# Attention scores as plain fp32 products of 64 rows, two units per visit, with mask and row maximum in one instruction

## The chip, the core and the metric

The kernel runs on one core of a Trainium2 chip. Five engines work side by side, each through its own queue in order: TensorE (PE, with weight loads listed apart as PEld), VectorE (DVE), ScalarE (ACT), GpSimd (POOL) and SyncE (SP), which here only issues DMAs. The metric is the device time of one execution in microseconds; the time given is the median of several.

## The reference

Sparse attention over 8 batches, 8 heads, 576 positions and 64 head dimensions, then a gated feed-forward layer on the 4608 tokens that result (512 to 1536 to 512):

```python
scores = scale * np.matmul(q, k.transpose(0, 1, 3, 2))        # scale = 1/8
mask_local = (rel >= 0) & (rel < 32)                          # heads 0-3
mask_strided = (rel >= 0) & (pos[None, :] % 32 == pos[:, None] % 32)   # heads 4-7
scores = np.where(masks, scores, -1000000000.0)
attn = np.exp(scores - np.max(scores, axis=-1, keepdims=True))
attn = attn / (np.sum(attn, axis=-1, keepdims=True) + 1e-09)
x = np.matmul(attn, v)                                        # tokens x 512
rms = np.sqrt(np.mean(x * x, axis=-1, keepdims=True) + 1e-06)
xn = x / rms * rms_g
g = xn @ w_gate
return (g * (1.0 / (1.0 + np.exp(-g))) * (xn @ w_val)) @ w_out
```

Everything is fp32.

## The kernel before

**Work.** The feed-forward layer goes through the tokens in nine chunks of 512: chunks 0 to 6 one at a time, the last two together by another scheme of products (lines 1190 to 1590). For one chunk, each of twelve slices of 128 hidden columns takes products for the gate (`g`), for the value (`v`) and for the output (`acc`), with 512 tokens as moving columns. A large fp32 product is written as three products in a rounded fp32 type, high times high, low times high and high times low (lines 970 and 1027); the two parts of each operand are made by a cast (`hi`) and a subtraction (`lo`).

**Attention.** The masks leave blocks only. A pair of heads is cut into three units, 96 units in all (`wus`, line 450; `o` is the number of the pair, three units to a pair, four pairs to a batch). A unit has two tiles, or one, for each of its two heads: local heads have tiles of 96 queries by 128 keys, strided heads tiles of 126 by 126 or 108 by 108. A unit runs through `step_s` (scores on PE, mask and row maximum on DVE, exponential on ACT, normalising on POOL), `step_t` (transposing, for most units on DVE in blocks of 32) and `step_o` (times the values on PE, then copies into `raw`, from which a chunk takes its tokens). Units 0 to 14 come in a prologue; from unit 15 on a unit is started with each slice of the chunk before, so that attention is spread between the large products.

**Scores before.** Two forms matter. Units 12 to 26 (line 653) multiply plain fp32 operands of 64 rows, the first head on rows 0 to 63 and the second on rows 64 to 127. From unit 27 on (`FP`, line 638) the operands are taken apart first: `split` (line 515) makes, for each pair of heads, six casts (line 540, ACT) and four subtractions (line 545, DVE) into the buffer `qk`, so that one product of 128 rows and 256 columns in the rounded type gives two of the three parts side by side. DVE then adds the mask to the first half (lines 674, 678), adds the second half (line 680) and takes the row maximum (line 681). For units 15 to 26 it adds the mask for each head (line 684) and takes the maximum (line 686).

**Buffers.** The buffer `qk` of `QKN` elements is also the place of three of the five slots for queries and keys (`xx`, line 387) until unit 27; after that there are only two slots, and each pair's scores come from `qk`. `pbuf` (the probabilities) has `NPB` = 2 buffers. Scores, transposes and values share one pair of PSUM banks, `pair`.

**Order.** Nothing is written in the order in which it runs. `op(...)` records an operation with its engine, cost, due time, and what it reads and writes; `Plan.order` (line 201) makes a schedule from the costs in two passes with the parameters `PASS_A` and `PASS_B` (`SWITCH` says where the second takes over), and each engine's instructions are emitted in that order. `also=` lists other engines that may take an operation, so a planner's choice can move work between DVE, POOL and ACT.

Of the kernel before, what the change touches and what calls it, by code (L numbers as in the profile page):

```python
# [343 lines left out]
def attn_moe(ctx: ExitStack, tc: tile.TileContext, qT: bass.AP, kT: bass.AP, vl: bass.AP, vs: bass.AP,  # L344
# [170 lines left out]
    def split(o, at):
        first = 3 * o == FP

        def part(fn, src, key, more=()):
            ways = [("ACT", act(S), False), ("DVE", 375, True)] if not more else [("DVE", 780, True), ("Pool", pool(S), True)]
            if "g" not in ALT:  # L520
                ways = ways[:1]
            op(*ways[0][:2], at, fn, reads=[("xx", src)] + list(more), writes=[key], port=ways[0][2], also=ways[1:])

        def begin():
            lw = sb.tile([P, QKN], F32R, name="qk")
            qk["q"] = lw[:, 0:2 * S].rearrange("p (h s) -> p h s", h=2)
            qk["k"] = lw[:, 2 * S:QKN].rearrange("p (h w s) -> p h w s", h=2, w=2)
            for h in range(2):
                for a, e in ((0, PAD), (SW, KP)):
                    z2 = ident[:, 0:2 * (e - a)].rearrange("p (w s) -> p w s", w=2)  # L530
                    nc.scalar.activation(out=qk["k"][:, h, :, a:e], in_=z2, func=AF.Copy, scale=0.0)
                r = (BOT, TOP)[h]
                nc.scalar.activation(out=qk["k"][r, h, 1, PAD:SW], in_=xx[1][r, PAD:SW], func=AF.Copy, scale=0.0)
        if first:
            op("ACT", 1800, at, begin, reads=[("xx", 1), "ident"],
               writes=low_keys + [(n, h, w) for n in "qk" for h in range(2) for w in range(3)])

        def copy(eng, d, s):
            if eng == "ACT":
                nc.scalar.copy(out=d, in_=s)  # L540
            else:
                (nc.gpsimd if eng == "Pool" else nc.vector).tensor_copy(out=d, in_=s)

        def sub(eng, d, s, y):
            (nc.gpsimd if eng == "Pool" else nc.vector).tensor_tensor(out=d, in0=s, in1=y.bitcast(F32), op=ALU.subtract)  # L545
        for h in range(2):
            r, z = ((TOP, BOT), (BOT, TOP))[h]
            q, k = (lambda r, h=h: qk["q"][r, h]), (lambda r, w, h=h: qk["k"][r, h, w, PAD:SW])
            x, y = xx[0][r, PAD:SW], xx[1][r, PAD:SW]
            part(lambda e, q=q, x=x, r=r: copy(e, q(r), x), 0, ("q", h, 0))  # L550
            part(lambda e, q=q, x=x, r=r, z=z: sub(e, q(z), x, q(r)), 0, ("q", h, 1), [("q", h, 0)])
# [1297 lines left out]
```

## Time and profile before

| | before |
|---|---|
| runs, us | 1011.88, 1016.63, 1017.29 (median 1016.63) |
| profiled execution, us | 1014.29, of which the span from first to last instruction is 1012.5 |
| mean granted TensorE clock | 0.994 |
| mean DMA rate over the span | 120 GB/s |

A group line of the profile gives line, engine, operation, what is written and read, shapes and count, then the busy time in us and the mean of one in ns, then the idle time of the engine just before. A timeline line gives the start and length in us, and in brackets how long the engine had been idle and who ended it. Matmuls overlap, so the length of one says little; the distance from one start to the next is its cost.

### The profile page before, as it was taken

How to read it: one execution, taken by the hardware profiler on the slowest of the kernel's cores; microseconds unless marked ns; L12 is line 12 of the kernel's file. 1: busy time of each engine (PE TensorE's matmuls, PEld its weight loads, DVE VectorE, ACT ScalarE, POOL GpSimd, SP SyncE). 2: the span in 40 equal slices, each digit the busy share in tenths (PEclk: the TensorE clock that was granted, in tenths of full speed). 3: DMA queues.
4: the chain of work that ended last, by engine and by line, in shares of the span. 5: the costliest groups of instructions: out<-in, count | busy, mean ns of one | idle time of the engine just before them, and what ended most of it. 6: DMA issues, size and time to landing. Idle time of an engine off the chain costs nothing.

```text
span 1012.5 us, 15391 instructions
## 1 busy us (share of the span) xinstructions
PE 992.7 (98%) x5104; PEld 805.4 (80%) x5104; DVE 846.3 (84%) x1745; ACT 572.1 (57%) x1502; POOL 416.6 (41%) x390
## 2 busy tenths in 40 slices
PE   8899998999999999999999999999999999999998
PEld 7678776788878888888878888887888878888886
DVE  5699999898889797779888888888987798888891
ACT  7899857655755456456555555555655444344440
POOL 6232457324562333533325342267643343565300
PEclk9899999999999999999999999999999999999999
DMA  9876342532442331433232432234322101120552
GB/s 310 294 271 225 134 138 96 169 116 85 159 146 81 114 122 60 166 99 112 92 120 91 136 114 98 88 122 140 108 91 79 42 0 42 42 84 1 158 165 73
DMA packets 52559, 121.11 MB, mean 120 GB/s; under 512 B 5312, under 2 KB 21248, under 8 KB 52480
## 3 DMA queue, kind: packets, MB, share of 16 engines
q1 hardware_dynamic: 51712, 119.28, 35.3%
q10 hardware_dynamic: 768, 0.85, 0.3%
q8 instruction: 40, 0.66, 0.3%
q14 instruction: 39, 0.32, 0.1%
HBM read 98.09 MB, written 22.02 MB: 119 GB/s over the span
## 4 chain that ended last, share of the span: by engine, by line
PE 81%; DVE 12%; ACT 4%; issue 2%; DMA 1%; DVEq 0%; ACTq 0%
PE g L970 18%; PE v L970 18%; PE acc L1027 18%; PE g L1356 3%; PE pair L1356 3%; PE v L1356 3%; PE pair L782 3%; PE pair L638 3%; DVE qk L545 2%; PE acc L1356 2%; PE g L1521 2%; PE v L1521 2%; PE acc L1521 2%; DVE raw L918 1%; DVE pT L745 1%
## 5 line engine op out<-in xcount | busy, mean ns | idle before, releaser
L970 PE MATMUL g<-xh,wg 128*128 128x512 f32 x672 | 211.8, 396 | 4.4 <-DVE e L985 4.4
L970 PE MATMUL v<-xh,wv 128*128 128x512 f32 x664 | 208.4, 395 | 1.8 <-DVE e L996 0.9
L1027 PE MATMUL acc<-or,hh 128*128 128x512 f32 x672 | 208.7, 392 | 0.0
L1012 POOL TENSOR_TENSOR hl<-e,hh 128x512 fp32r<-128x512 f32 x84 | 115.3, 1372 | 216.8 <-ACT hh L1003 196.4
L693 ACT ACTIVATE pp<-pp,mx 96x128 f32<-96x128 f32 (+2 forms) x296 | 114.2, 390 | 74.5 <-DVE mx L681 60.7
L702 POOL TENSOR_TENSOR pp<-pp,mx 96x512 f32<-96x512 f32 (+3 forms) x87 | 88.3, 1017 | 156.4 <-DVE mx L699 106.3
L970 PEld LDWEIGHTS g<-xh,wg 128*128 128x128 f32 x672 | 122.4, 189 | 31.1 <-DVE e L985 5.0
L1027 PEld LDWEIGHTS acc<-or,hh 128*128 128x128 f32 x672 | 124.4, 188 | 26.5 <-ACT ssq L1038 0.4
L970 PEld LDWEIGHTS v<-xh,wv 128*128 128x128 f32 x664 | 121.9, 189 | 28.7 <-DVE e L996 2.6
L970 PE MATMUL g<-xl,wg 128*128 128x512 f32 x336 | 131.9, 393 | 0.2 <-POOL xl L946 0.2
L1027 PE MATMUL acc<-or,hl 128*128 128x512 f32 x336 | 130.9, 390 | 0.0
L970 PE MATMUL v<-xl,wv 128*128 128x512 f32 x332 | 129.6, 390 | 0.0
L745 DVE STREAM_TRANSPOSE pT<-pp 32x128 f32<-32x128 f32 (+1 forms) x376 | 109.7, 292 | 11.9 <-POOL pp L702 6.9
L1003 ACT CAST hh<-e 128x512 fp32r<-128x512 f32 x84 | 52.4, 624 | 89.5 <-PE acc L1027 80.5
L983 ACT ACTIVATE e<-g 128x512 f32<-128x512 f32 x84 | 50.1, 597 | 78.6 <-PE g L970 64.4
L540 ACT CAST qk<-xx 64x576 fp32r<-64x576 f32 x138 | 88.8, 670 | 5.3 <-PE pair L638 3.8
L545 DVE TENSOR_TENSOR qk<-xx,qk 64x576 fp32r<-64x576 f32 x92 | 83.0, 902 | 6.3 <-ACT qk L540 3.8
L985 DVE SCALAR_TENSOR_TENSOR e<-e,g 128x512 f32<-128x512 f32 x84 | 57.4, 683 | 27.4 <-ACT e L983 26.5
L970 PEld LDWEIGHTS g<-xl,wg 128*128 128x128 f32 x336 | 63.4, 189 | 14.6 <-POOL xl L946 0.6
L1027 PEld LDWEIGHTS acc<-or,hl 128*128 128x128 f32 x336 | 63.1, 188 | 13.5
L970 PEld LDWEIGHTS v<-xl,wv 128*128 128x128 f32 x332 | 62.5, 188 | 13.4
L996 DVE SCALAR_TENSOR_TENSOR e<-e,v 128x512 f32<-128x512 f32 x83 | 56.9, 685 | 14.5 <-PE v L970 10.5
(515 smaller groups left out, 1804.7 us busy)
## 6 DMA issues: line engine op xcount, KB each, us to landing
or<-wos SPq DMA_DIRECT2D x72, 512.0 KB, 3.3
xx<-in_qT_dram SPq DMA_DIRECT2D x26, 288.0 KB, 2.8
xx<-in_kT_dram SPq DMA_DIRECT2D x25, 288.0 KB, 3.9
wg<-in_wgv_dram SPq DMA_DIRECT2D x12, 512.0 KB, 9.6
vt<-in_vl_dram SPq DMA_DIRECT2D x16, 384.0 KB, 3.2
wv<-in_wgv_dram SPq DMA_DIRECT2D x12, 512.0 KB, 7.4
or<-in_wo_dram SPq DMA_DIRECT2D x12, 512.0 KB, 4.2
wos<-or SPq DMA_DIRECT2D x12, 512.0 KB, 3.0
```

Of the source, the lines that this page charges most:

```text
L540: nc.scalar.copy(out=d, in_=s)
L545: (nc.gpsimd if eng == "Pool" else nc.vector).tensor_tensor(out=d, in0=s, in1=y.bitcast(F32), op=ALU.subtract)
L693: nc.scalar.activation(out=pv[:, h, x], in_=sp[h][:, x] if i < PM else pv[:, h, x], func=AF.Exp, scale=0.125 if i < PM else 1.0, bias=mx[: ...
L702: (nc.vector if e == "DVE" else nc.gpsimd).tensor_tensor(out=pv, in0=pv, in1=mx.unsqueeze(3).broadcast_to([m, 2, nt, n]), op=ALU.mult)
L745: nc.vector.transpose(out=dst[32 * y:32 * y + 32, :, 32 * x:32 * x + 32], in_=src[32 * x:32 * x + 32, :, 32 * y:32 * y + 32])
L970: nc.tensor.matmul(out=out, lhsT=wt[:, w, sl], rhs=xhl[x, kc], start=(kc == 0 and i == 0), stop=(kc == KC - 1 and i == 2))
L985: op("DVE", dve(CH), at + MO, lambda: nc.vector.scalar_tensor_tensor(out=e, in0=e, scalar=1.0, in1=bank["g"], op0=ALU.add, op1=ALU.mult), ...
L996: op("DVE", dve(CH), at + MO, lambda: nc.vector.scalar_tensor_tensor(out=e, in0=e, scalar=0.5, in1=bank_of(c, ("v", u))[0], op0=ALU.mult, ...
L1012: (nc.vector if n == "DVE" or h else nc.gpsimd).tensor_tensor(out=hl[h], in0=e, in1=hh[h].bitcast(F32), op=ALU.subtract)
L1027: nc.tensor.matmul(out=acc[t], lhsT=x[h][:, sl], rhs=wt[:, w], start=(u == 0 and i == 0), stop=(u == NU - 1 and i == 2))
L1356: nc.tensor.matmul(out=banks[bk], lhsT=w, rhs=X[a, k].tile(y), start=start and k == 0 and i == 0, stop=stop and k == 1 and i == 2, skip_gr ...
L1521: nc.tensor.matmul(out=banks[bks[j]], lhsT=tile(v, k, j), rhs=x.tile(y), start=start and k == 0 and i == 0, stop=stop and k == KT - 1 and ...
```

## The change

Units from 27 on no longer take their operands apart. `FP` is 99 and the code behind it is gone: `split`, the buffer `qk`, the products of line 638, the three or four DVE instructions of lines 674 to 681. All units from 12 on use the products of line 653 (line 604 after). From unit 28 (`BT`) on, two units are scored in one visit of PE: the second's scores stand in columns 256 to 511 of the two banks, and the visit therefore also takes the bank halves of transposes and values (`("T", 0)`).

For units from 15 on, mask, scale, and row maximum are one `tensor_tensor_reduce` for each head and tile. It computes -0.125 times the sum of score and mask (the mask is 0 or -1e9, so it stays far below all scores after the scaling) and keeps the minimum, which is the negative of the row maximum; the exponential then runs with scale -1.

The slots for queries and keys become six buffers of their own, `pbuf` has four, the last pair of chunks places its operands in `xx2` to `xx5` and `pp2`, `pp3` where it had `qk`, and planner numbers differ.

```diff
+TTRC = 135.0
+SC0 = 272.0
-FP = 27
+FP = 99
+BT = 28
-BA = 30000.0
-BM = 60000.0
+BA = 10000.0
+BM = 20000.0
-NPB = 2
+NPB = 4
-PASS_A = ([25.0, 0.0, 150.0, 50.0], 0.2, 8000.0, 12)
-PASS_B = ([25.0, 600.0, 300.0, 400.0], 0.2, 12000.0, 5)
-SWITCH = 220000.0
+PASS_A = ([25.0, 0.0, 150.0, 37.5], 0.3, 4000.0, 8)
+PASS_B = ([25.0, 900.0, 225.0, 300.0], 0.2, 4000.0, 7)
+SWITCH = 180000.0
...
-    low = sbt([P, QKN], "qk")
-    xx = [sbt([P, SW], f"xx{i}") for i in range(2)] + [low[:, SW * i:SW * i + SW] for i in range(3)]
+    xx = [sbt([P, SW], f"xx{i}") for i in range(6)]
...
-            starts[s] = [i]
+            starts.setdefault(s - (i >= BT and (i - BT) % 2), []).append(i)
...
     def slot_of(o, x):
-        return x if 3 * o >= FP else (2 * o + x) % 5
+        return (2 * o + x) % 6
...
-    def step_s(i):
+    def step_s(i, part=None):
...
-        sp = [pair[:m, h, 0:nt * n].rearrange("q (t k) -> q t k", k=n) for h in range(2)]
+        off = 256 * ((i - BT) % 2) if i >= BT else 0
+        sp = [pair[:m, h, off:off + nt * n].rearrange("q (t k) -> q t k", k=n) for h in range(2)]
+        SKS = [SK] if i < BT else [SK, ("T", pn)]
...
             for h in range(2):
-                nc.vector.scalar_tensor_tensor(out=pv[:, h], in0=sp[h], scalar=0.125, in1=mk, op0=ALU.mult,
-                                               op1=ALU.add)
-            nc.vector.tensor_reduce(out=mx, in_=pv, axis=AX.X, op=ALU.max, negate=True)
+                for x in range(nt):
+                    nc.vector.tensor_tensor_reduce(out=pv[:, h, x], in0=sp[h][:, x], in1=mk[:, x], scale=-0.125, scalar=3.0e38,
+                                                   op0=ALU.add, op1=ALU.min, accum_out=mx[:, h, x:x + 1])
...
-                                         scale=0.125 if i < PM else 1.0,
+                                         scale=0.125 if i < PM else -1.0,
...
+            def scores_of(units):
...
+                if units[0] >= BT:
+                    todo = [step_s(i, True) for i in units]
+                    op("PE", SC0 + sum(x[2] for x in todo), at + PE_S, lambda: [x[0]() for x in todo], reads=[y for x in todo for y in x[1]],
+                       writes=[("S", 0), ("T", 0)], lock=("b0", "b1"))
+                for i in units:
+                    step_s(i)
```

Three places of the order show how it moves instructions. On **PE**, in the second chunk, units 30 and 31 (a pair of strided heads) before; `g` and `v` are the gate and value products, `acc` the output products:

```order
L970 MATMUL g_68<-xl0_475,wg4_911 128x512
L638 MATMUL pair_72<-qk_1686 126x256 x4
L970 MATMUL g_68<-xh1_523,wg4_911 128x512 x2
L970 MATMUL g_68<-xl1_531,wg4_911 128x512
...
L1027 MATMUL acc01_70<-or0_1737,hl0_749 128x512
L638 MATMUL pair_72<-qk_1686 108x256 x4
L970 MATMUL v_69<-xh2_580,wv4_935 128x512 x2
```

and the same two units after:

```order
L966 MATMUL acc23_71<-or1_1783,hl0_758 128x512
L604 MATMUL pair_72<-xx3_79,xx2_78 126x126 x4
L604 MATMUL pair_72<-xx3_79,xx2_78 108x108 x4
L909 MATMUL g_68<-xh0_498,wg1_656 128x512 x2
L909 MATMUL g_68<-xl0_516,wg1_656 128x512
```

Two visits of four products of 256 columns became one visit of eight products of 126 or 108 columns, and the operands are the loaded queries and keys themselves.

On **DVE**, a piece of the second chunk before: the four subtractions of `split` for one pair of heads, with the gate's two instructions (`e`) between them, and the mask, second half and maximum of one unit:

```order
L545 TENSOR_TENSOR qk_1686<-xx0_77,qk_1686 64x576
L545 TENSOR_TENSOR qk_1686<-xx1_78,qk_1686 64x576
L985 SCALAR_TENSOR_TENSOR e_94<-e_94,g_68 128x512
L545 TENSOR_TENSOR qk_1686<-xx0_77,qk_1686 64x576
L996 SCALAR_TENSOR_TENSOR e_94<-e_94,v_69 128x512
L545 TENSOR_TENSOR qk_1686<-xx1_78,qk_1686 64x576
...
L678 SCALAR_TENSOR_TENSOR pp0_89<-pair_72,cb_64 126x4x126
L680 SCALAR_TENSOR_TENSOR pp0_89<-pair_72,pp0_89 126x4x126
L681 TENSOR_REDUCE mx2_101<-pp0_89 126x4
```

and one unit after, at the start of the second chunk (`ISA` is the new instruction; it stands with a second one that writes only the maximum, `mx`):

```order
L857 SCALAR_TENSOR_TENSOR raw1_74<-raw1_74,few_66,srt_1688 128x512
L624 ISA pp0_92,mx0_104<-pair_72,cb_64 96x128
L624 ISA mx0_104 96x1
L624 ISA pp0_92,mx0_104<-pair_72,cb_64 96x128
L624 ISA mx0_104 96x1
...
L684 STREAM_TRANSPOSE pT0_96<-pp2_94 32x4x32 x3
```

The subtractions are gone, and three instructions for a unit became four pairs of a long and a very short one.

On **SP**, in the prologue, the load of the fifth pair's keys before (`qk` holds slots 2 to 4; `wg`, `wv`, `or` are weights):

```order
L579 DMA qk_76<-in_qT_dram 128x576
L1633 DMA wg2_125<-in_wgv_dram 128x1024
L1633 DMA wv2_126<-in_wgv_dram 128x1024
L1633 DMA wg3_127<-in_wgv_dram 128x1024
L597 DMA vt0_79<-in_vs_dram 126x2x320
L579 DMA qk_76<-in_kT_dram 128x576
L1633 DMA wv3_128<-in_wgv_dram 128x1024
```

and after:

```order
L1570 DMA wv0_127<-in_wgv_dram 128x1024
L536 DMA xx3_79<-in_kT_dram 128x576
L536 DMA xx5_81<-in_kT_dram 128x576
L536 DMA xx1_77<-in_kT_dram 128x576
L1570 DMA wg1_128<-in_wgv_dram 128x1024
L536 DMA xx0_76<-in_qT_dram 128x576
```

The keys of the fifth pair (`xx3`), and those of the next two, are issued ahead of all weights but the first two; before, the fifth pair's keys came behind seven of them.

More of the change, by code (lines that the diff above doesn't have):

```diff
@@ L72 @@
 EVS = (0,)
-KP = 32 + 596
-QKN = 2 * 576 + 4 * KP
 EQ = (('ACT', 'DVE'), ('ACT', 'DVE'))
@@ L438, in attn_moe @@
         op("DVE", 300, -1, lambda: nc.vector.memset(ebuf, 0.0), writes=["wz", "e"])
-    for x in range(5):
+    for x in range(6):
         op("Pool", 100, -1, lambda x=x: nc.gpsimd.memset(xx[x][:, 0:PAD], 0.0), writes=[("xp", x)])
@@ L512, in slot_of @@
     def slot_of(o, x):
-        return x if 3 * o >= FP else (2 * o + x) % 5
[L515 to L551, printed above, removed]
-            part(lambda e, k=k, y=y, r=r: copy(e, k(r, 0), y), 1, ("k", h, 0))
-            part(lambda e, k=k, y=y, z=z: copy(e, k(z, 0), y), 1, ("k", h, 2))
-            part(lambda e, k=k, y=y, r=r: sub(e, k(r, 1), y, k(r, 0)), 1, ("k", h, 1), [("k", h, 0)])
@@ L632, in scores @@
         def scores():
-            if i >= FP:
-                for x, t in enumerate(tl):
-                    q0 = LQ * t if p < 2 else NROW * RES0[t]
-                    k0 = q0 if p < 2 else q0 + PAD
-                    for h in range(2):
-                        nc.tensor.matmul(out=pair[:m, h, 256 * x:256 * x + 256], lhsT=qk["q"][:, h, q0:q0 + m],
-                                         rhs=qk["k"][:, h, :, k0:k0 + P], start=True, stop=True)
-                return
             if i < PM:
@@ L654, in scores @@
                                          start=i >= PM, stop=i >= PM or x == nt - 1)
-        op("PE", (PF if i < n_pro else 1) * (2 * nt * (10 + 1.67 * n) + (250 + 0.84 * nt * n) * (i < PM)) if i < FP else 2 * nt * 120,
-           at + PE_S, scores, reads=([("xa", qs)] + [("wa", kz_key(0, h)) for h in range(2)] if o == 0 else []) + ([("xx", qs)] if i else []) + [("xp", ks)] + ([("xx", ks)] if o >= KZ else [(n, kz_key(o, h)) for h in range(2) for n in ("w", "kz") if i or n == "kz"]) + ["cb", ("hl", 0)] * (i < PM) if i < FP else [(n, h, w) for n in "qk" for h in range(2) for w in range(2 + (n == "k"))],
-           writes=[SK] if i < FP - 1 else [SK, ("T", pn)], lock=locks)
+        rd = ([("xa", qs)] + [("wa", kz_key(0, h)) for h in range(2)] if o == 0 else []) + ([("xx", qs)] if i else []) + [("xp", ks)] + (
+            [("xx", ks)] if o >= KZ else [(n, kz_key(o, h)) for h in range(2) for n in ("w", "kz") if i or n == "kz"]) + ["cb", ("hl", 0)] * (i < PM)
+        if i < BT:
+            op("PE", 2 * nt * (10 + 1.67 * n) + (250 + 0.84 * nt * n) * (i < PM) if i < n_pro else SC0 + 2 * nt * (0.84 * n + 2),
+               at + PE_S, scores, reads=rd, writes=[SK], lock=locks)
+        if part:
+            return scores, rd, 2 * nt * (0.84 * n + 2)
         def rowmax():
@@ L1201, in lazy @@
             return fresh[tag, dt]
-        qk_keys = [(n, h, w) for n in "qk" for h in range(2) for w in range(2 + (n == "k"))]
-        old = {"qk": qk_keys, f"raw{free_raw}": [("raw", free_raw, k) for k in range(KC)]}
+        old = {f"raw{free_raw}": [("raw", free_raw, k) for k in range(KC)]}
         for i in range(2):
             old[f"vt{i}"] = [("vt", i)]
+            old[f"pp{i + 2}"] = [("pp", i + 2)]
+        for x in range(2, 6):
+            old[f"xx{x}"] = [("xx", x), ("xp", x)]
         old["ssq"], old["srt"] = ["ssq"], ["srt"]
@@ L1709, in attn_moe @@
             begin = starts.get(NU * c + u, [])
[L1711 to L1719 removed]
+            def scores_of(units):
+                for i in units:
+                    b, p, j = wus[i]
+                    if j == 0:
+                        load(b, p, at_of(i) - 2 * unit)
+                        if i < PP0:
+                            load_v(b, p, at_of(i) - 2 * unit)
+                if units[0] >= BT:
+                    todo = [step_s(i, True) for i in units]
+                    op("PE", SC0 + sum(x[2] for x in todo), at + PE_S, lambda: [x[0]() for x in todo], reads=[y for x in todo for y in x[1]],
+                       writes=[("S", 0), ("T", 0)], lock=("b0", "b1"))
+                for i in units:
+                    step_s(i)
             def values_of(units):
```

58 lines of the change are left out of this document (7 added, 51 removed), and 2 rows, old and new, of the table xplace.

## The prediction

> **What bounds the kernel now.** I read the page first, then PE by stages, PE's waits in the two stages with idle time, and single visits in the timeline.
>
> ```profile
> span 1012.5 us, 15391 instructions
> ...
> PE 992.7 (98%) x5104; PEld 805.4 (80%) x5104; DVE 846.3 (84%) x1745; ACT 572.1 (57%) x1502; POOL 416.6 (41%) x390
> ```
>
> PE is busy for 98% of the span. So an edit can win at most what PE still waits, and each nanosecond that it adds to PE's own work is paid in full unless a wait goes for it. The windows (columns: stretch, then busy time of PE, PEld, DVE, ACT, POOL, granted clock, DMA share, GB/s) say where PE waits: the prologue, chunk 0 in two parts, and chunks 1 to 6 up to the last unit's scores.
>
> ```profile
> 0.00:52.00 52.00, 45.85 (x349) 36.15 (x350) 32.05 (x103) 41.96 (x161) 24.29 (x45) 0.93 0.90 302
> 52.00:143.00 91.00, 90.62 (x501) 70.94 (x500) 87.47 (x162) 81.13 (x199) 34.32 (x27) 1.00 0.56 193
> 143.00:182.00 39.00, 33.97 (x160) 25.70 (x159) 38.18 (x71) 27.28 (x67) 24.02 (x21) 0.96 0.35 127
> 182.00:780.00 598.00, 594.38 (x3087) 487.70 (x3086) 505.51 (x1130) 332.06 (x921) 250.97 (x235) 1.00 0.34 112
> ```
>
> From 143 to 182 us PE idles 39.00 - 33.97 = 5.0 us while DVE is busy 38.18 of 39; the clock there is 0.96, so about 39 x 0.04 = 1.5 us more go to a slow clock after the waits. From 182 to 780 it idles 3.6 us. The waits of PE in these two stages, first 143 to 182, then 182 to 780 (total us, times, longest):
>
> ```profile
> PE g L970 <- DVE e L985: 2.6, 1, 2.6
> ...
> PE v L970 <- DVE wv L1670: 0.8, 1, 0.8
> ```
>
> ```profile
> PE g L970 <- DVE e L985: 1.4, 2, 1.0
> PE pair L638 <- DVE qk L545: 0.9, 2, 0.5
> ```
>
> Nearly all are waits for DVE at the start of a chunk, or for `split` itself.
>
> **PE's own work grows by about 5.4 us.** The timeline around a visit of the old form (line 638) and between two large products:
>
> ```profile
> 300.98 0.39 PE L970 MATMUL g<-xl,wg 128*128 128x512 f32 x1
> 301.21 0.62 PE L970 MATMUL v<-xh,wv 128*128 128x512 f32 x2
> ...
> 309.48 0.40 PE L1027 MATMUL acc<-or,hl 128*128 128x512 f32 x1
> 309.71 0.64 PE L638 MATMUL pair<-qk 128*126 128x256 f32 x4
> 310.19 0.64 PE L970 MATMUL g<-xh,wg 128*128 128x512 f32 x2
> ```
>
> A large product takes 0.23 us, also ahead of the visit, so entering it is free; four old products take 310.19 - 309.71 = 0.48 us, 0.12 each. There are 252 of them (units 27 to 95): 30.2 us. The new form runs already, for units 12 to 26; three visits:
>
> ```profile
> 109.13 0.39 PE L970 MATMUL g<-xl,wg 128*128 128x512 f32 x1
> 109.45 0.63 PE L653 MATMUL pair<-qk 64*108 64x108 f32 x8
> 110.01 0.73 PE L970 MATMUL g<-xh,wg 128*128 128x512 f32 x2
> ```
>
> ```profile
> 118.83 0.39 PE L970 MATMUL g<-xl,wg 128*128 128x512 f32 x1
> 119.15 0.44 PE L653 MATMUL pair<-qk 64*108 64x108 f32 x4
> 119.52 0.73 PE L1027 MATMUL acc<-or,hh 128*128 128x512 f32 x2
> ```
>
> ```profile
> 145.20 0.39 PE L970 MATMUL g<-xl,wg 128*128 128x512 f32 x1
> 145.52 0.68 PE L653 MATMUL pair<-qk,xx 64*96 64x128 f32 x8
> 146.13 0.73 PE L970 MATMUL v<-xh,wv 128*128 128x512 f32 x2
> ```
>
> Each product is two records. From the large product ahead to the one behind, less its own 0.23: four products of 108 columns cost 0.65, two cost 0.46, four of 128 columns 0.70. Two products of 108 are thus 0.19, or 0.095 each; a fixed 0.46 - 0.19 = 0.27 is left for each visit; and 128 columns are (0.70 - 0.27)/4 = 0.107. For 126 columns I scale to 0.105. The 252 products are 132 of 128 columns (11 local pairs), 48 of 126 and 72 of 108 (12 strided pairs): 14.1 + 5.0 + 6.8 = 25.9 us. Visits: unit 27 alone, then 68 units in 34: 35 x 0.27 = 9.5. Together 35.4 against 30.2, **+5.2**; with rounding of the 0.12, +4 to +6.5. Without the merging it would be 69 x 0.27 = 18.6 and +14.3, so "two units per visit" carries the change. [...]
>
> **DVE and ACT lose work.** Groups by line (before):
>
> ```profile
> L540 ACT CAST qk<-xx 64x576 fp32r<-64x576 f32 x138 | 88.8, 670 | 5.3 <-PE pair L638 3.8
> L545 DVE TENSOR_TENSOR qk<-xx,qk 64x576 fp32r<-64x576 f32 x92 | 83.0, 902 | 6.3 <-ACT qk L540 3.8
> ...
> L680 DVE SCALAR_TENSOR_TENSOR pp<-pair,pp 96x512 f32<-96x512 f32 (+3 forms) x69 | 42.7, 619 | 2.4
> L681 DVE TENSOR_REDUCE mx<-pp 96x4 f32<-96x512 f32 (+3 forms) x69 | 42.4, 615 | 2.4
> ...
> L678 DVE SCALAR_TENSOR_TENSOR pp<-pair,cb 96x512 f32<-96x512 f32 (+3 forms) x58 | 34.8, 600 | 5.2 <-PE pair L638 2.9
> ...
> L698 DVE TENSOR_REDUCE mx<-su 96x4 f32<-96x8 f32 (+3 forms) x96 | 14.6, 152 | 13.6 <-ACT pp L693 10.8 <-ACT xh L693 1.7 <-ACT xl L693 0.3
> ...
> L674 DVE SCALAR_TENSOR_TENSOR pp<-pair,cb 96x256 f32<-96x256 f32 x22 | 8.3, 413 | 0.8 <-PE pair L638 0.4
> L684 DVE SCALAR_TENSOR_TENSOR pp<-pair,cb 96x256 f32<-96x256 f32 (+3 forms) x24 | 8.1, 378 | 0.5 <-issue 0.4
> ...
> L686 DVE TENSOR_REDUCE mx<-pp 96x4 f32<-96x512 f32 (+3 forms) x12 | 7.4, 618 | 0.4
> ```
>
> Removed: 88.8 us on ACT; on DVE 83.0 of subtractions and 8.3 + 34.8 + 42.7 + 42.4 + 8.1 + 7.4 = 143.7 of masks and maxima. Added: one pair of instructions for each head and tile of units 15 to 95, 252 + 44 = 296. The trace has no such instruction. The nearest rows are the mask additions, which read PSUM and the mask too: for each form apart, and two in a row in the timeline:
>
> ```profile
> L678 DVE SCALAR_TENSOR_TENSOR pp<-pair,cb 96x512 f32<-96x512 f32 x22 | 15.0, 683 | 1.8 <-PE pair L638 1.3
> ```
>
> ```profile
> 151.04 0.75 DVE L684 SCALAR_TENSOR_TENSOR pp<-pair,cb 96x256 f32<-96x256 f32 x2
> ```
>
> 512 elements take 0.68 us and 256 take 0.41 (line 674), so 128 take about 0.41 - 0.27/2 = 0.28. From above, the short second instruction waits for the first and costs a whole 0.15 (line 698): 0.43. From below, it costs nothing and the long ones overlap as the two above do (0.75 instead of 2 x 0.41, 0.07 each): 0.21. I take 0.29, in which both overlap like the row above: 0.28 - 0.07 + 0.15 - 0.07. That is 86 us (62 to 127), so DVE falls by 141 us (100 to 165) of 846.
>
> [...]
>
> All of this lies beside a busy PE and is worth only the waits it removes. What is late next is the chain inside a chunk's start (square sums, root, gain, split into two parts), which the change leaves as it is.
>
> **What PE may get back.** First, the prologue, in the chain that ended last and in the timeline:
>
> ```profile
> 20.91 8.86 DMA qk<-in_kT_dram
> ```
>
> ```profile
> 29.91 0.68 PE L653 MATMUL pair<-qk 64*96 64x128 f32 x8 [2.18 <-DMA qk<-in_kT_dram]
> ```
>
> The fifth pair's keys go to a slot that the third pair's queries hold, so they are issued at 20.9 us and PE waits 2.2 us for them. With six slots they go to an unused one, ahead of most weights. ACT and DVE must follow, since both also work in this stage (41.96 and 32.05 of 52): I take 2.2, between 0 and 3. On SP the three early loads push weights back by under 0.9 MB, about 3 us at 302 GB/s; the weights' own conversion hides this as long as DVE, not DMA, paces chunk 0 (87.47 of 91 against a DMA share of 0.56). If that cover fails, the 2.2 are gone.
>
> Second, chunk 1's start: 6.5 us with the slow clock. The last wait there ended so:
>
> ```profile
> 163.15 3.87 DVE L918 SCALAR_TENSOR_TENSOR raw<-raw,few,srt 128x512 f32<-128x512 f32 x2
> ```
>
> Two instructions of some 0.7 us took 3.87, on a DVE that had nothing else. That is not DVE load but a stretched instruction, and the new schedule may or may not have it again. The ACT and DVE work of the first `split` lies just here and goes. I take 4, between 0 and 6.5. Third, chunks 1 to 6: 0.9 us of waits for `split` go surely, the rest of 3.6 in part: I take 2.5, between 0.9 and 3.6. Merged visits hold the bank `pair` through eight maxima instead of one unit's, 8 x 0.29 = 2.3 us, but such visits are some 17 us apart, and the planner has four buffers now: no cost taken, up to 2 us.
>
> **Sum.** 5.2 - 2.2 - 4 - 2.5 = -3.5. The profiled execution took 1014.29 us (span 1012.5), so 1010.8 by it; its place is 2.3 below the median of the runs, 1016.63, by which it would be 1013.1. I say **1012**, 0.45% under the median. A measurement of this kernel can tell about 0.5% (5 us) from no change.
>
> **Rivals.**
> 1. *All waits go.* With a DVE relieved by a sixth, both later stages close: 5.2 - 3 - 6.5 - 3.6 = -7.9, some 1007. For it: nearly every wait names DVE. Against it: the stretched `raw` instruction, and chunk starts are latency.
> 2. *The pair of instructions is dear.* At 0.43 it is above the 15.5 us / 44 = 0.352 that units 15 to 26 pay now for each product, so DVE, busy 96 to 98% of chunk 0, gets 44 x 0.08 = 3.4 us more where PE already waits for it, and those waits do not go: 5.2 - 2.2 - 0.9 + 3.4 = +5.5, about 1021, slower. It decides from 0.352 up. For it: no row shows the instruction. Against it: DVE instructions overlap in the row above.
> 3. *PE's price without a return.* New waits take the place of those removed (a burst of eight exponentials, weights that come later): 5.2 in full, 1019.5 by the profiled execution.
> 4. *The two heads do not run side by side.* Then 25.9 us double: +26, about 1040. Against it: four products end within 0.70 us in the visit above, in the same alternation that the new visits have.
>
> **How the numbers follow.** The forecast, between -1 and -5: 0.43. Rival 1, with what lies between it and the forecast: 0.38. Rivals 2 and 3: 0.17, rival 4: 0.02. Faster by over 0.5% is rival 1 and the low end of the forecast, 0.40; slower by over 0.5% is rivals 2 to 4 as far as they pass +5, 0.14; the rest, 0.46, is no change. The range is 1003 to 1020: below by rival 1 with a run as low as the lowest shown (1011.88 - 7.9 = 1004), above by PE's full price with nothing returned (1014.29 + 5.2 = 1019.5).
>
> **What would show it.** Line 604's visits of eight products should take 0.27 + 8 x 0.107 = 1.13 us between large products. The new DVE pair should stand about 0.29 us apart. PE's wait for `xx` from `in_kT_dram` at 30 us should be gone, and PE's idle time in the 39 us around chunk 1's start and in chunks 1 to 6 should be about half. DVE should be near 705 us and ACT near 483. [...]

## The result, and the profile after

Twenty executions of the changed kernel took 1019.43 us in the median (1014.93 to 1022.18), twenty of the kernel before 1015.62 (1011.88 to 1018.69). The ratio is 1.0036 with an interval of 1.0025 to 1.0047: the change costs some 3.7 us. The profiled execution took 1019.23 us, the one of before 1014.29. One of the eleven executions of e13_head below took 1644.1 us at a mean clock of 0.556 and is left out of its ratio.

The page of the changed kernel, its span and the busy time of each engine:

```profile
span 1017.4 us, 15890 instructions
...
PE 999.3 (98%) x5356; PEld 803.9 (79%) x5356; DVE 690.5 (68%) x1985; ACT 484.7 (48%) x1357; POOL 420.9 (41%) x400
```

DVE lost 155.8 us and ACT 87.4. PE, which sets the time, shows 6.6 us more. The windows of the changed kernel (columns as before: stretch, busy time of PE, PEld, DVE, ACT, POOL, granted clock, DMA share, GB/s), with the same edges as those of before and the tail added:

```profile
0.00:52.00 52.00, 46.66 (x344) 36.92 (x344) 29.79 (x97) 40.09 (x161) 24.33 (x48) 0.87 0.91 300
52.00:143.00 91.00, 90.23 (x507) 70.17 (x507) 85.17 (x219) 84.72 (x204) 35.99 (x28) 1.00 0.57 201
143.00:182.00 39.00, 33.46 (x191) 24.31 (x189) 38.15 (x112) 23.06 (x67) 29.13 (x24) 1.00 0.39 129
182.00:780.00 598.00, 597.98 (x3299) 483.40 (x3296) 360.90 (x1313) 248.10 (x777) 230.07 (x220) 1.00 0.33 111
780.00:1017.00 237.00, 230.96 (x1024) 189.10 (x1022) 176.53 (x248) 88.75 (x149) 101.39 (x82) 1.00 0.21 67
```

The tail of the kernel before, which the prediction didn't show:

```profile
780.00:1012.00 232.00, 227.85 (x1014) 184.86 (x1012) 183.10 (x283) 89.65 (x161) 83.02 (x64) 1.00 0.21 68
```

What PE loses in a stretch is its idle time (length less busy time) and what the slow clock takes (by an estimate, length times what the clock lacks to 1). The last column belongs to a kernel of the experiments, whose rows stand below:

| stretch, us | before | changed | e13_head |
|---|---|---|---|
| 0 to 52: idle + clock | 6.2 + 3.6 | 5.3 + 6.8 | 5.3 + 1.6 |
| 52 to 143 | 0.4 | 0.8 | 1.2 |
| 143 to 182 | 5.0 + 1.6 | 5.5 + 0 | 2.7 + 0 |
| 182 to 780 | 3.6 | 0.0 | 0.8 |
| 780 to the end | 4.2 | 6.0 | 5.0 |
| all losses | 24.6 | 24.4 | 16.6 |
| span less losses: PE's own work | 987.9 | 993.0 | 993.8 |

The clock has two digits in these rows, so a few tenths in the first stretches and up to 3 us in the long one are rounding; the shares of the whole span's mean clock (0.994, 0.992 and 0.998) give 6, 8 and 2 us of slow clock, within 1.5 us of the table. With this the table is the profiled pair in small. What remains for PE's own work grew by 5.1 us. What PE loses is as much as before in sum: 3.6 us went from 182 to 780 us and 1.1 around chunk 1's start, and 2.3 came in the first 52 us, 0.4 behind them and 1.8 in the tail. In idle time alone PE loses 17.6 us in place of 19.4, 1.8 less, and in slow clock 1.6 more.

The extra slow clock belongs to these two executions. Over the executions with a clock on record it averages 6.8 us in both kernels (87 executions of the kernel before, run with the experiments, and 20 of the changed kernel; span times what the mean clock lacks to 1). What the change costs, it costs in PE's work and idle time: the time less the slow clock is 1012.6 us in the mean against 1009.4.

PE's waits of the changed kernel in its first 60 us, and the timeline and the clock around the first of them:

```profile
PE pair L600 <- DMA xx<-in_qT_dram: 1.8, 1, 1.8
PE v L435 <- DVE few L426: 1.5, 1, 1.5
PE pair L695 <- DVE mx L620: 0.7, 1, 0.7
```

```profile
20.41 0.38 PE L594 MATMUL pair<-cb,hl 126*126 126x252 bf16 x2
22.56 0.76 PE L600 MATMUL pair<-wg,xx 128*126 128x126 f32 x2 [1.77 <-DMA xx<-in_qT_dram]
23.11 0.63 PE L600 MATMUL pair<-wv,xx 128*126 128x126 f32 x2
```

```profile
20.00:24.00 4.00, 2.22 (x14) 2.00 (x14) 1.59 (x6) 2.31 (x10) 2.47 (x2) 0.80 1.02 400
24.00:28.00 4.00, 4.00 (x26) 3.76 (x26) 2.00 (x7) 2.68 (x13) 1.68 (x2) 0.50 1.05 337
28.00:32.00 4.00, 4.00 (x29) 3.40 (x30) 1.37 (x5) 1.83 (x9) 0.62 (x1) 0.50 1.04 362
```

The wait for keys at 29.9 us is gone. A wait for the queries of pair 3 stands 7 us earlier, where DMA is busy all the time (a share of 1.02 to 1.05 in these rows), and behind it PE runs for 8 us at half clock (two records of a product take 0.63 us here, and 0.38 in e15 below, where the clock is whole). In this execution the wait of 1.8 us has 0.8 + 2 + 2 = 4.8 us of slow clock behind it.

### The profile page after: what moved, and what is told of

It is laid out like the page before. It is cut to its first block, busy times and chain, and to the rows that moved or that the text cites. A ratio compares the mean times of both kernels' runs of the same rounds, so it can differ in the third digit from the quotient of the medians.

```text
span 1017.4 us, 15890 instructions
## 1 busy us (share of the span) xinstructions
PE 999.3 (98%) x5356; PEld 803.9 (79%) x5356; DVE 690.5 (68%) x1985; ACT 484.7 (48%) x1357; POOL 420.9 (41%) x400
## 4 chain that ended last, share of the span: by engine, by line
PE 90%; DVE 7%; issue 1%; ACT 1%; DMA 1%; DVEq 0%; ACTq 0%
PE g L909 22%; PE v L909 21%; PE acc L966 21%; PE pair L604 4%; PE g L1295 3%; PE pair L721 3%; PE v L1295 3%; PE pair L1295 3%; PE g L1460 2%; PE acc L1460 2%; PE v L1460 2%; PE acc L1295 1%; PE pair L1460 1%; DVE pT L684 1%; DMA xx<-in_qT_dram 1%
## 5 line engine op out<-in xcount | busy, mean ns | idle before, releaser
L641 POOL TENSOR_TENSOR pp<-pp,mx 96x512 f32<-96x512 f32 (+3 forms) x87 | 84.2, 975 | 109.7 <-DVE mx L638 64.7
L624 DVE CUSTOM_DVE_ANT_0 pp<-pair,cb 96x128 f32<-96x128 f32 (+2 forms) x296 | 65.6, 277 | 10.2 <-PE pair L604 8.3
L632 ACT ACTIVATION_READ_ACCUMULATOR pp<-pp,mx 96x1 f32 (+2 forms) x296 | 55.8, 188 | 0.0
```

The costliest lines, as they stand in the source:

```text
L624: nc.vector.tensor_tensor_reduce(out=pv[:, h, x], in0=sp[h][:, x], in1=mk[:, x], scale=-0.125, scalar=3.0e38, op0=ALU.add, op1=ALU.min, ac ...
L632: nc.scalar.activation(out=pv[:, h, x], in_=sp[h][:, x] if i < PM else pv[:, h, x], func=AF.Exp, scale=0.125 if i < PM else -1.0, bias=mx[ ...
L641: (nc.vector if e == "DVE" else nc.gpsimd).tensor_tensor(out=pv, in0=pv, in1=mx.unsqueeze(3).broadcast_to([m, 2, nt, n]), op=ALU.mult)
```

## Experiments

All kernels with the new form and merged visits give PE the same products; what differs is the order that the planner makes. Where an edit shows planner numbers, they are PASS_A, PASS_B, SWITCH, BA and BM as in the change. In all that follows a ratio is to the kernel before, run on the same chip.

**e1_late_k: the early key loads behind the queries.** The load of a key tile of pairs 4 to 6 gets one more predecessor for the planner, pair 3's queries:

```
-                   writes=[("xx", s) if z or len(parts) == 1 else ("xa", s)], bytes_=P * (e1 - a) * 4)
+                   reads=[("xx", 0)] if x and o in (4, 5, 6) else [], writes=[("xx", s) if z or len(parts) == 1 else ("xa", s)], bytes_=P * (e1 - a) * 4)
```

> Changed kernel with one order changed: the key loads of pairs 4, 5 and 6 (0.86 MB, issued from 11.85 us by the changed kernel) are issued behind the query load of pair 3. Theory (early key loads push pair 3's queries back; PE waits 1.8 us for them at 20.8 us and then runs at clock 0.50 from 24 to 32 us): that wait goes, the clock of the first 52 us rises from 0.87 to 0.93 or more, and the time falls by 3 to 5 us to about 1015. Rival (the prologue is paced by weights and DVE; a later start there is caught up in chunk 0): the wait goes and the time stays at 1019.

Measured: 1021.96 us, ratio 1.0058 (1.0037 to 1.0080); not better than the change as made, whose interval overlaps with this one. PE's waits in the first 60 us:

```profile
PE pair L721 <- DMA vt<-in_vs_dram: 3.1, 1, 3.1
PE pair L695 <- DVE mx L620: 1.7, 1, 1.7
```

The wait for queries went, as expected, and one of 3.1 us for pair 3's values took its place. The clock of the first 52 us rose to 0.93 and the idle time with it, to 8.7 us, and the time didn't fall: the rival. The profiled execution, at a mean clock of 0.995, is no typical one here; the median of the six is 0.9905, against 0.993 for the changed kernel, so over its executions e1 has no gain in clock.

**e7_k_as_before: the key loads where they stood before**, behind the values (the same edit, with `("vt", (o > 4) + 0)` as the predecessor).

> Changed kernel with the key loads of pairs 4 to 6 where the kernel before issued them: pair 4's behind pair 2's values, pair 5's and 6's behind pair 3's values. Theory (DMA is busy for 0.9 of the first 30 us, so whichever load is put last is waited for; the early key loads only moved the wait from keys to queries, and behind the queries to values): PE waits about 2 us for keys again, at about 28 us, no wait for queries or values over 0.8 us, and PE's loss in the first 52 us is that of before, 2 us less than the changed kernel's. Rival (the wait comes from somewhere else): a wait of 1.5 us or more for queries or values stays. The time is 1016 to 1024, since the planner moves later work with it.

Measured: 1023.22 us, ratio 1.0065 (1.0048 to 1.0083).

```profile
PE pair L604 <- DMA xx<-in_kT_dram: 3.6, 1, 3.6
```

Now it is the keys again, and longer than before. Queries in the changed kernel, values in e1, keys here: in these three profiles, with a DMA share of 0.91, 0.93 and 0.89 over the first 52 us, a load that is put late is waited for. Two parts of the expectation did not hold: queries are waited for too, 1.0 us, and the stretch does not have before's loss, since PE idles 10.6 us there.

**e2_single and e6_single_visits: the merging alone undone** (`BT = 99`).

> Changed kernel without the merging: every unit from 28 on has a visit of its own, so 34 visits more. Theory (a visit of 64-row products costs PE a fixed 0.27 us, whatever is in it): 34 x 0.27 = +9.2 us, about 1028.5, and PE busy about 1008. Rival (the fixed cost belongs to the neighbour or is hidden): within 2 us of 1019.

> Changed kernel without the merging, every unit from 28 on with a visit of its own (34 visits more), and with each visit holding both halves of the bank pair as merged visits do. Theory (a visit costs PE a fixed 0.27 us): PE's own work up by 9.2 us, 1028.5 by that alone; 1029 to 1034 with the 0 to 5 us that an order not fitted to it adds. Rival (a visit's fixed cost is hidden): under 1022.

Both took longer than expected. In e2 a visit doesn't hold the bank `pair` against the values of other units, so a part of the attention is overwritten; it took 1033.71 us, ratio 1.0181 (1.0161 to 1.0201). In e6 it holds it: 1036.41 us, ratio 1.0195 (1.0176 to 1.0213). A merged visit of the changed kernel in the timeline, of eight products in 16 records, and then a single one of e6 with four:

```profile
331.63 0.39 PE L909 MATMUL g<-xl,wg 128*128 128x512 f32 x1
331.95 1.12 PE L604 MATMUL pair<-xx,xx 64*96 64x128 f32 x16
333.00 0.74 PE L966 MATMUL acc<-or,hh 128*128 128x512 f32 x2
333.58 0.40 PE L966 MATMUL acc<-or,hl 128*128 128x512 f32 x1
```

```profile
310.10 0.39 PE L909 MATMUL v<-xl,wv 128*128 128x512 f32 x1
310.42 0.71 PE L604 MATMUL pair<-xx,xx 64*126 64x126 f32 x8
311.06 0.74 PE L909 MATMUL g<-xh,wg 128*128 128x512 f32 x2
```

The first takes 333.00 - 331.63 - 0.23 = 1.14 us (1.13 was predicted), the second 0.73. Over all visits from 185 to 780 us, added up in the same way from one start to the next, the changed kernel spends 33.3 us on 232 products in 32 visits and e6 41.9 us on 232 products in 64: 8.6 / 32 = 0.27 us for a visit, the predicted value.

This way of adding up stops at the start of the large product behind the visit, and so did the prediction's. But that product is late as well. Behind the visit above, two large products take 333.58 - 333.00 = 0.58 us. Behind a visit of the old form, in the kernel before, two take 310.66 - 310.19 = 0.47:

```profile
310.19 0.64 PE L970 MATMUL g<-xh,wg 128*128 128x512 f32 x2
310.66 0.39 PE L970 MATMUL g<-xl,wg 128*128 128x512 f32 x1
```

The 0.11 us are there behind every visit of the new form from 182 to 780 us (0.34 us from the first large product to the second in the mean of 33 visits, against 0.23 in the mean of 69 visits of the old form). A visit costs 0.27 + 0.11 = 0.38 us. For e6 that is 32 x 0.11 = 3.5 us on top of the 8.6, of the 17.0 by which it is above the changed kernel. Most of the other 5 us shows in its profile as losses around chunk 1's start: from 143 to 182 us PE idles 6.3 us and the clock is 0.91, against 5.5 and 1.00.

**e3_old_plan and e5_before_new_plan: form and planner numbers crossed.** Beside the form, the change replaces five planner numbers. e3 is the changed kernel with the old ones (the edit below), e5 the kernel before with the new ones (the same lines the other way round):

```
-BA = 10000.0
-BM = 20000.0
+BA = 30000.0
+BM = 60000.0
-PASS_A = ([25.0, 0.0, 150.0, 37.5], 0.3, 4000.0, 8)
-PASS_B = ([25.0, 900.0, 225.0, 300.0], 0.2, 4000.0, 7)
-SWITCH = 180000.0
+PASS_A = ([25.0, 0.0, 150.0, 50.0], 0.2, 8000.0, 12)
+PASS_B = ([25.0, 600.0, 300.0, 400.0], 0.2, 12000.0, 5)
+SWITCH = 220000.0
```

> Changed kernel with the planner's numbers of before (BA, BM, PASS_A, PASS_B, SWITCH). Theory (the planner's numbers move waits about, but neither the price on PE nor the early key loads): 1017 to 1021, with the wait for the queries at about 21 us still there. Rival (the new numbers made the new waits in chunk 1's start and in the tail): about 3 us less, 1016, and PE idles under 3 us from 143 to 182 us.

> Kernel before, with the changed kernel's five planner numbers (BA, BM, PASS_A, PASS_B, SWITCH) and nothing else of the change. Theory (each set of numbers is fitted to its own form; an order that is not fitted costs 5 to 10 us in waits and slow clock, as the changed kernel with the old numbers showed with 1028): 1021 to 1026, PE's idle time and slow clock of the page up by that much. Rival (the new numbers are better or worse by themselves): under 1014, so that the old form with them would beat both kernels, or over 1030.

| us | old numbers | new numbers |
|---|---|---|
| old form | 1015.6 | 1028.0 (ratio 1.0117, 1.0097 to 1.0137) |
| new form | 1028.1 (ratio 1.0126, 1.0107 to 1.0146) | 1019.4 |

Each form loses 9 to 12 us with the other's numbers. For e3 that was more than either theory had; for e5 it was the theory's side, a little above its range. The waits of e5 behind the first 60 us begin with these:

```profile
PE g L970 <- ACT xh L931: 7.3, 3, 4.3
PE g L856 <- POOL ssq L851: 1.9, 1, 1.9
```

So no number "is" the time of a form; each form has a time in one order, and 3.7 us is less than what an order can cost.

**e4_old_mask: mask and maximum in the old way.**

```
-            for h in range(2):
-                for x in range(nt):
-                    nc.vector.tensor_tensor_reduce(out=pv[:, h, x], in0=sp[h][:, x], in1=mk[:, x], scale=-0.125, scalar=3.0e38,
-                                                   op0=ALU.add, op1=ALU.min, accum_out=mx[:, h, x:x + 1])
+            for h in range(2):
+                nc.vector.scalar_tensor_tensor(out=pv[:, h], in0=sp[h], scalar=0.125, in1=mk, op0=ALU.mult, op1=ALU.add)
+            nc.vector.tensor_reduce(out=mx, in_=pv, axis=AX.X, op=ALU.max, negate=True)
...
-                                         scale=0.125 if i < PM else -1.0,
+                                         scale=0.125 if i < PM else 1.0,
```

> Changed kernel with mask, scale and maximum as in the old form for plain products: two scalar_tensor_tensor and one tensor_reduce for a unit instead of one tensor_tensor_reduce for each head and tile. By the rows (0.41 + 0.41 + 0.62 against 4 x 0.21 for a unit of two tiles) DVE gets 0.6 us more for 81 units, about 45 us, to 735. Theory (from 182 us on PE waits for nothing, so DVE time is free there; in chunk 0, where DVE is busy for 85 of 91 us, 12 units x 0.6 = 7 us count in part): +1 to +4 us, 1020 to 1023. Rival (the relief of DVE is what closed the waits of chunks 1 to 6): those waits come back, +4 to +8.

Measured: 1027.12 us, ratio 1.0113 (1.0092 to 1.0134); DVE 738.5 us, 48 more than the changed kernel. PE's waits behind the first 60 us:

```profile
PE pair L604 <- DVE pp L623: 8.3, 3, 4.3
PE g L909 <- DVE e L924: 2.6, 2, 2.5
```

The waits didn't come back in chunks 1 to 6 (from 182 to 780 us PE is busy for 597.0 of 598), as the rival had it, but in chunk 1's start, where DVE is full: from 143 to 182 us PE is busy for 28.95 of 39 at clock 0.82. The size is the rival's; the place is neither's, since the theory had chunk 0. How much of the 8 us is DVE's work and how much an order that doesn't fit it is not told apart.

**e8_plan_a to e11_plan_b3: other orders for the same form.** The planner's numbers alone are changed, with its price of one maximum (`TTRC`) set to what the trace shows; e9 to e11 differ from e8 in PASS_B only:

```
-TTRC = 135.0
+TTRC = 77.0
...
-BA = 10000.0
-BM = 20000.0
+BA = 15000.0
+BM = 30000.0
...
-PASS_A = ([25.0, 0.0, 150.0, 37.5], 0.3, 4000.0, 8)
-PASS_B = ([25.0, 900.0, 225.0, 300.0], 0.2, 4000.0, 7)
-SWITCH = 180000.0
+PASS_A = ([25.0, 100.0, 150.0, 100.0], 0.3, 4000.0, 10)
+PASS_B = ([25.0, 1200.0, 150.0, 300.0], 0.2, 12000.0, 6)
+SWITCH = 150000.0
```

That is e8. PASS_B is `([25.0, 900.0, 150.0, 300.0], 0.2, 4000.0, 5)` in e9, `([25.0, 900.0, 150.0, 300.0], 0.2, 12000.0, 7)` in e10 and `([25.0, 900.0, 225.0, 300.0], 0.2, 8000.0, 8)` in e11.

> Changed kernel with another set of planner numbers (PASS_A, PASS_B, SWITCH, BA, BM) and the price of one maximum set to the 0.21 us that the trace shows. Theory (the new form needs about 5 us more of PE than the old one, and the rest of the time is what the order loses in waits and slow clock, about 25 us in both kernels): a better order can win part of that back, 1014 to 1020, with PE's own work unchanged. Rival (the 25 us are bound by transfers and the chains at the chunks' starts, whatever the order): 1019 to 1022.

> The kernel of e8_plan_a with another PASS_B, which orders only what starts after the first 150 us. Theory (in e8_plan_a one wait of 4.0 us at the last chunk's start, at 817 us, behind DVE instructions of two to three times their usual length, is what keeps it above the kernel before; the first 780 us are as good as before's in spite of 5 us more PE work): another order there has a wait of another length, and without it the time is 1014, between 1013 and 1019. Rival (such a wait comes back at each order of the tail): 1018 as in e8_plan_a.

> As e9_plan_b1 with a third PASS_B. Theory: the same head up to about 150 us and a saturated PE from 182 to 780 us, so that only the waits from 780 us on differ; 1013 to 1019. Rival: 1018 as in e8_plan_a, with a wait of 3 us or more in the tail again.

> As e9_plan_b1 with a fourth PASS_B. Theory: 1013 to 1019 by the waits from 780 us on alone. Rival: 1018 as in e8_plan_a, with a wait of 3 us or more in the tail again.

| kernel | median us | ratio (interval) |
|---|---|---|
| e8_plan_a | 1018.11 | 1.0021 (1.0010 to 1.0033) |
| e9_plan_b1 | 1015.05 | 0.9996 (0.9981 to 1.0010) |
| e10_plan_b2 | 1022.49 | 1.0065 (1.0051 to 1.0078) |
| e11_plan_b3 | 1015.69 | 1.0001 (0.9986 to 1.0016) |

e8's wait of 4.0 us at 817 us is 1.8 at the most in e9 and e11, and e9 comes out at before's time. e10, with the head of the others, has waits of 6.2 us in the line for `e` and 1.8 more in the tail, so such waits do come back with some orders. The times of e8, e9 and e11 are in their theories' ranges; e10's is above theory and rival.

**e12_before_plan_c: another order for the old form** (PASS_A `([25.0, 0.0, 75.0, 50.0], 0.25, 4000.0, 12)`, PASS_B `([25.0, 900.0, 225.0, 400.0], 0.2, 4000.0, 7)`, SWITCH 140000, BA 15000, BM 30000).

> Kernel before with another set of its planner's numbers (PASS_A, PASS_B, SWITCH, BA, BM), as e8_plan_a to e11_plan_b3 are for the changed kernel. Theory (the form sets PE's work, 5 us less in the old form than in the new one; the order sets the losses, 20 to 40 us, and of the old form one order has been shown that loses 13 us more than the kernel before): between 1013 and 1026, with all of the difference from before in PE's idle time and slow clock. Rival (the old form stays near 1016 at any well-made order): within 2 us of 1016.

Measured: 1016.34 us, ratio 0.9999 (0.9983 to 1.0015). The rival holds at this order: the old form has two orders at 1016, as the new one so far has two at 1015 to 1016.

**e13_head and e14_tail: which half of the order.** e13 is e9 with the changed kernel's PASS_B, which orders what starts behind the first 150 us; e14 is the changed kernel with e9's PASS_B.

> e9_plan_b1's numbers (PASS_A, SWITCH, BA, BM, price of a maximum) with the changed kernel's PASS_B, so that the order of the first 150 us is that of e9_plan_b1. Theory (the changed kernel loses its 4 us up to 182 us, 3.3 of it by the slow clock in the first 52 us): 1014 to 1018. Rival (PASS_B, which orders what starts later, makes the difference): 1019 or more.

> The changed kernel with e9_plan_b1's PASS_B alone, so that the order of its first 180 us stays. Theory: 1018 to 1021, with the wait for queries at 20.8 us and the slow clock behind it still there. Rival (PASS_B makes the difference): 1016 or less.

e13: 1013.49 us, ratio 0.9980 (0.9970 to 0.9991). e14: 1020.65 us, ratio 1.0041 (1.0026 to 1.0056). The numbers that come with the head (PASS_A, SWITCH, BA, BM and the price of a maximum, not told apart) make the difference, with either PASS_B, and **e13 is faster than both kernels**, by 2 us than the kernel before. It is the best of eight orders tried for the new form, against three for the old one. Its windows, and its longest waits in the first 60 us:

```profile
0.00:52.00 52.00, 46.70 (x380) 36.55 (x380) 37.34 (x116) 43.69 (x162) 25.66 (x49) 0.97 0.96 322
52.00:143.00 91.00, 89.81 (x487) 69.96 (x485) 85.08 (x203) 78.98 (x190) 40.72 (x32) 1.00 0.58 198
143.00:182.00 39.00, 36.30 (x170) 27.32 (x169) 33.98 (x78) 22.36 (x55) 22.09 (x19) 1.00 0.46 161
182.00:780.00 598.00, 597.25 (x3333) 480.98 (x3333) 369.16 (x1359) 249.56 (x794) 231.04 (x223) 1.00 0.32 107
780.00:1010.00 230.00, 224.98 (x1001) 184.88 (x995) 175.31 (x242) 88.81 (x150) 101.16 (x76) 1.00 0.21 69
```

```profile
PE v L435 <- DVE few L426: 1.5, 1, 1.5
PE pair L721 <- ACT xl L699: 1.0, 2, 0.6
PE acc L841 <- DVE few L836: 0.5, 1, 0.5
```

In the first 52 us PE idles 5.3 us, no less than in the changed kernel, but behind the start in pieces of under 0.7 us, and the clock is 0.97 instead of 0.87. SP issues the early key loads ahead of pair 3's queries here too; PE comes to them at 21.45 us and finds them landed. From 143 to 182 us DVE has 34 us of work instead of 38, and PE idles 2.7 us instead of 5.5. One thing did not come as expected: e14's profiled execution, with the changed kernel's head, has no wait above 0.3 us for the queries and a clock of 0.97 in the first 52 us; it was the fastest of its five (1018.02). That wait is there in some executions of this order and not in others.

**e15_fill: the wait filled.** Two idle products stand in PE's order where the changed kernel waits for the queries (`i == 9` is pair 3's first unit; their bank is overwritten later):

```
-                    nc.tensor.matmul(out=sp[h], lhsT=identb[:m, :m], rhs=mk, start=True, stop=False)
+                    nc.tensor.matmul(out=sp[h], lhsT=identb[:m, :m], rhs=mk, start=True, stop=False); [nc.tensor.matmul(out=bank["g"], lhsT=ones, rhs=ebuf, start=True, stop=True) for _ in range(2 * h * (i == 9))]
```

> The changed kernel with two products of 128x512 more, at the place in PE's order where it waits 1.8 us for pair 3's queries; their results are overwritten, and nothing else in the order changes. Theory (the wait costs PE its clock: 0.50 from 24 to 32 us after it, some 4 us): the two products fill most of the wait, the clock of the first 52 us rises from 0.87 to 0.93 or more, and the time falls by 2 to 4 us, to 1015 to 1017.5. Rival 1 (the slow clock is covered by other waits for DMA and DVE in the prologue): the clock rises and the time stays at 1018 to 1020. Rival 2 (the slow clock has another cause): the clock stays and the two products are paid, 1019 to 1021.

Measured: 1017.41 us, ratio 1.0017 (1.0004 to 1.0030), 2.0 us under the changed kernel's 1019.43. That is the small end of the theory's range, and the gain is barely clear of noise, since the two intervals of ratios overlap; rival 1's 1018 to 1020 isn't excluded by the time, but rival 2 is by the clock. The timeline and the clock of e15 at that place:

```profile
21.57 1.88 PE L594 MATMUL g<-e,ones 128*128 128x512 f32 x4
24.25 0.45 PE L600 MATMUL pair<-wg,xx 128*126 128x126 f32 x2 [0.80 <-DMA xx<-in_qT_dram]
24.54 0.38 PE L600 MATMUL pair<-wv,xx 128*126 128x126 f32 x2
```

```profile
24.00:28.00 4.00, 3.75 (x38) 3.54 (x38) 1.91 (x7) 2.23 (x11) 1.19 (x2) 1.00 1.04 377
28.00:32.00 4.00, 3.64 (x43) 2.62 (x42) 3.20 (x8) 3.83 (x20) 1.51 (x2) 1.00 1.05 303
0.00:52.00 52.00, 43.99 (x351) 33.63 (x351) 32.36 (x99) 41.21 (x163) 23.90 (x48) 0.97 0.97 309
```

The queries land 1.7 us later here than in the changed kernel's profile, and still the clock holds at 1.00 up to 32 us. The mean clock of the whole span, in the median of the executions, is 0.993 for the changed kernel and for e14, which has its head and ran with e15, 0.9965 for e15 and 0.9975 for e13: 7.1, 3.6 and 2.5 us of slow clock. It is 0.993 for the kernel before too. So e15 has 3.5 us less of slow clock, against which stands what of its 1.9 us of products lies outside the wait; 2.0 were measured. And of the 5.9 us by which e13 is under the changed kernel, 4.6 are clock.

## Why the prediction was off

A time of 1012 us was forecast, 4.6 under the median then known; the change costs 3.7 us instead. Of its sum, 5.2 - 2.2 - 4 - 2.5, the three returns make 8.7 us. The idle time fell by 1.8, and over the executions the slow clock did not fall at all. The first term was too small as well.

- **PE's own work: the visit is dearer than 0.27 us.** +5.2 was predicted and 5.1 stands in the table, but the agreement is partly luck. The 1.14 us for a merged visit and the 0.27 for each are as predicted; the 0.11 us behind each visit are not in the sum, and 35 x 0.11 = 3.9 us bring it to about 9. The prediction's own rows show them: the two large products behind each visit have 0.73 us there, and 0.64 behind the old form's. The table has only 5.1, because it counts as work whatever is not idle: beside the waits of the kernel before from 182 to 780 us, large products start up to 0.5 us apart, which makes 2.3 us more than their usual distance, against 0.5 us in the changed kernel. Where the rest of the difference between 9 and 5.1 lies is not shown. Rival 4 is out: the 25.9 us of products did not double, since eight of them and their visit take 1.14 us.
- **DVE and ACT: right in kind, the new instruction cheaper still.** In the changed kernel's timeline the maxima of two heads read:

```profile
417.19 0.08 DVE L624 DVE_READ_ACCUMULATOR2_ANT mx<- 126x1 f32 x1
417.19 0.28 DVE L624 CUSTOM_DVE_ANT_0 pp<-pair,cb 126x126 f32<-126x126 f32 x1
417.40 0.08 DVE L624 DVE_READ_ACCUMULATOR2_ANT mx<- 126x1 f32 x1
417.40 0.28 DVE L624 CUSTOM_DVE_ANT_0 pp<-pair,cb 126x126 f32<-126x126 f32 x1
```

  One starts 0.21 us after the other, the low end of the predicted 0.21 to 0.43 (0.29 was taken). The read-out of 0.08 us lies wholly beside the next maximum. So rival 2 is out. If each waited for the end of the one before, the same rows would give 0.28 + 0.08 = 0.36. DVE came to 690.5 us where 705 were predicted.
- **Chunks 1 to 6: right.** All 3.6 us of idle time went; 2.5 were predicted.
- **The prologue's gain of 2.2 us: failed, 0.8 came in idle time.** The prediction had the keys "issued ahead of most weights" and asked only what the weights would lose by it. It did not ask what else stood behind those loads on SP; pair 3's queries did, and the wait for keys became, in the profiled execution, a wait of 1.8 us for queries. It also priced a wait at its own length. In the profiled pair the stretch lost 3.2 us more in slow clock, so 2.3 more in all; over all executions the span as a whole has neither more nor less of it than before. What e15 and e13 show is that clock can be won in this stretch: their profiles have 0.97 there against 0.87, and by their median clocks they have 3.5 and 4.6 us less of slow clock.
- **Chunk 1's start, 4 us: the step that failed most.** The idle time there rose from 5.0 to 5.5 us. The 1.1 us by which the profiled execution comes out lower are clock, 1.00 instead of 0.96, and e1, e14 and e15, with nearly the same work of PE there (33.5 to 33.9 us), show 0.96 again. The prediction held the chain and a stretched `raw` instruction for the cause, and the ACT and DVE work of the first `split` for something that lies there and goes. In the changed kernel DVE is as full as before in those 39 us (38.15 against 38.18), because the order puts other work there. The sums of the exponentials are one instruction for each unit; first before, then the changed kernel, from 143 to 182 us:

```profile
L698 DVE TENSOR_REDUCE mx<-su 96x4 f32<-96x8 f32 (+1 forms) x3 | 0.4, 118 | 0.0
```

```profile
L637 DVE TENSOR_REDUCE mx<-su 96x4 f32<-96x8 f32 x6 | 0.9, 146 | 0.1
```

  Six units in place of three. In e13, whose order has three there, DVE is free for 5 us, and PE's idle time halves. That the freed DVE is the cause of this was not tried apart. A stretched instruction is back as well, another one than the prediction's: the longest wait of PE there is for a subtraction that took 1.75 us (last section):

```profile
PE g L909 <- DVE xl L885: 2.0, 1, 2.0
```

- **The tail: not in the sum.** One new wait of 1.8 us there was not foreseen; e9, in another order, is without it, but has waits for another instruction (`e`: three behind the first 60 us, 4.1 us in all, 1.8 the longest). The new wait:

```profile
PE v L1295 <- DVE hh L1347: 1.8, 1, 1.8
```

Rival 3, PE's price without a return, gave 1019.5, and 1019.43 was measured. That they agree so closely is partly luck: 1019.5 starts from one execution of the kernel before, 1014.29, and from its median of 1015.62 the same 5.2 give 1020.8. Its mechanism is what happened in part: most of the waits removed were replaced by new ones, while PE's price was higher than 5.2. That the change loses is no property of the form: e13 has the same form and takes 5.9 us less than the changed kernel, 4.6 of them clock.

What stays open: why the queries land in time in some executions of one order and late in others, what sets the length of the slow clock behind a wait, how much PE's work grew between the table's 5 us and the 9 counted by visits, and whether the old form has an order at e13's time; two orders of it were near 1016 and one at 1028.

## What to carry to other kernels

With the bounding engine at 98%, price an edit by two sums, that engine's own work and its losses by stage, clock included; here 155.8 us less of DVE and 87.4 less of ACT came with 1.8 us less of idle time on PE, and around chunk 1's start the planner filled the relief with other work (DVE 38.15 us after, 38.18 before). When a load is moved forward in a full DMA stretch (a share of 0.91 here), list every load that it passes and who waits for each of them. When a visit's price is read off a timeline, look one product further than its end. And compare two forms only with several orders of each: here one order differed from another by up to 12 us, while the best ones shown for the two forms lie under 3 us apart.

## What was not expected of the hardware

- A wait of TensorE of 1.8 us at 20.8 us was followed by a clock of 0.50 up to 32 us, though PE was busy all that time; in e13 as much idle time in pieces of under 0.7 us (behind the start) left it at 0.97 over the first 52 us. In e15, with two idle products in the wait, it stayed at 1.00 up to 32 us. In these profiles the length of a wait doesn't set the loss. Behind the wait of 1.8 us 5.1 us of slow clock follow in all (22 to 34 us), behind 2.2 us for keys in the kernel before 1.7 (30 to 36 us), behind 1.7 us for DVE in e15 1.7 (32 to 40 us); e1, whose longest wait is 3.1 us, loses 3.6 in its first 52 us. And e13 loses 1.7 (32 to 40 us) with no wait above 0.65 us in front of it, the start aside.
- The accumulator's read-out (0.08 us) and the next `tensor_tensor_reduce` start together: 0.21 us from one to the next, though the two show 0.36 us of busy time.
- From the first large product behind a visit of the new form it is 0.34 us to the second, though both are of the usual kind, 0.23 us apart elsewhere. Behind the products with the values it is 0.34 in both kernels, behind the old form's visits 0.23.
- A subtraction took 1.75 us on DVE instead of 0.68 while POOL ran one of the same line:

```profile
171.00 1.71 POOL L885 TENSOR_TENSOR xl<-raw,xh 128x512 fp32r<-128x512 f32 x1
171.51 1.75 DVE L885 TENSOR_TENSOR xl<-raw,xh 128x512 fp32r<-128x512 f32 x1
...
174.74 0.68 DVE L885 TENSOR_TENSOR xl<-raw,xh 128x512 fp32r<-128x512 f32 x1
```

  The wait of 2.0 us of PE in the changed kernel's start of chunk 1 ended with it. That POOL is the cause was not tried.
